# A cached-attention decode step with a gated mixer: mixer moved and cut into pieces, value products collected by four heads, repeated weight loads dropped

## The chip, the cores and the metric

The kernel runs on one core of one Trainium2 chip. The metric is the device time of one execution in microseconds (us), as a median over several runs. The span in a profile, from the first to the last instruction, is about 1.8 us shorter than that time. Not all rounds ran on the same chip.

Engines: PE is TensorE (matmuls), PEld its weight loads, DVE is VectorE, ACT is ScalarE, SP issues most loads.

## The reference, cut to what matters

One token attends to 32 heads of 16384 cached keys and values (128 wide, bf16), and a small gated mixer is added to the result:

```python
q = (x @ wq) per head                        # x: 1 x 512
scores = q . k_cache * 128 ** -0.5           # 32 heads x 16384 keys x 128
o = softmax(scores) @ v_cache                # 32 heads x 16384 values x 128
a = concat(o) @ wo
z = gelu(x @ w_in); z1, z2 = halves of z     # 512 x 1792
b = (z1 * (w_sp * layernorm(z2) + b_sp)) @ w_out
g = sigmoid(sum(x * gate_w))
return g * a + (1 - g) * b
```

Every key and value is used once: 2 x 134 MB of cache plus some 11 MB of weights are read, 279.58 MB in all.

## The kernel before

Each head has a 4 MB key tile and a 4 MB value tile, 32 KB in each of the 128 SBUF partitions. There are three key buffers and two value buffers. DVE multiplies a key tile by the query, TensorE sums the products over the head dimension with identity weights, DVE reduces what is left, ACT takes the exponential, and TensorE multiplies the values. SP issues a load as soon as its buffer is free (in the chain of before the value load at 141.92 us comes 0.02 us after the last matmul on its buffer).

```python
def load_k(h):
    t = kv.tile([P, NJ * Dh], BF16, name="k_t", tag="k", bufs=3)
    nc.sync.dma_start(out=t[:], in_=k_src[h])
...
eps_t = const.tile([P, 1], FP32, name="eps_t")       # a constant tile; it matters below
...
def scores_half(h, s):                                # two halves per head
    nc.vector.tensor_tensor(out=ks, in0=ks, in1=qh, op=ALU.mult)      # 4.4 us
    for i in range(NS):                               # 16 matmuls, all with weights ident
        nc.tensor.matmul(s_ps[:, :, :], lhsT=ident[:, :], rhs=ks[:, :, i * W:(i + 1) * W], ...)
    nc.vector.tensor_reduce(out=s_sb[...], in_=s_ps[:, :, :], axis=AX.X, op=ALU.add)
    if s == 1: nc.scalar.activation(out=p_t[:], in_=s_sb[:], func=ACT.Exp, ...)

def attend_wide(h):                                   # 32 matmuls of 4 x 512, one copy
    for g in range(NG):
        nc.tensor.matmul(d_ps[:, :], lhsT=p_sb[h][:, g * R:(g + 1) * R],
                         rhs=vtile[h][:, g * R * Dh:(g + 1) * R * Dh], ...)
    nc.scalar.copy(out=d_sb[:], in_=d_ps[:, :])
def collect(h):                                       # 4 small matmuls per head
    ...
with tc.manual_schedule(engines={PE}):                # program order on PE, DVE left to the scheduler
    for h in range(H - 1):
        ... load_k(h + AHEAD); load_v(h)
        scores_half(h + AHEAD, 0); collect(h - 1); scores_half(h + AHEAD, 1); attend_wide(h)
        if h == 1:
            gate()
            mixer()
```

The two large mixer weights (2.75 MB) are loaded right after the first value tile. The last three heads use 128 matmuls of one column each in place of `attend_wide`, and the 4 MB of output weights come last, in four pieces.

The softmax here doesn't subtract the row's maximum and nothing guards it: scores larger than these inputs give would overflow.

## Time and profile before

| | before |
|---|---|
| time, median of 5 | 662.9 us |
| span in the profile | 661.8 us |
| read from HBM | 279.58 MB, 422 GB/s over the span |
| PE, PEld, DVE, ACT busy | 80%, 35%, 50%, 6% |

The page of the kernel before: the first two lines are busy tenths of the DMA engines and GB/s in 40 equal slices, then two DMA queues (packets, MB, share of the 16 engines), then the chain that ended last by engine, then three groups (busy us, mean ns of one, idle before it and what ended the idle time).

```profile
DMA  9999999899999999999999999999999999999996
GB/s 380 440 417 444 418 441 427 360 425 440 429 426 441 426 431 434 427 434 427 432 437 426 433 434 425 436 425 438 429 430 436 429 430 435 428 433 430 431 414 250
...
q1 hardware_dynamic: 10520, 279.58, 98.5%
q8 instruction: 22, 0.36, 0.2%
...
DMA 60%; PE 30%; DVE 9%; SPq 1%; issue 0%; ACT 0%; DVEq 0%
...
L222 DVE TENSOR_TENSOR k_t<-k_t,qb 128x8192 bf16<-128x8192 bf16 x64 | 280.5, 4421 | 137.1 <-DMA k_t<-in_A_k_cache_dram 137.1
L225 PE MATMUL s_ps<-k_t,ident 128*128 128x512 bf16 x1024 | 268.6, 423 | 95.3 <-DVE k_t L222 95.3
...
L225 PEld LDWEIGHTS <-ident 128*128 128x128 bf16 x1024 | 106.4, 107 | 243.4 <-issue 148.7
```

The DMA engines are busy nearly all the time, and the compute engines wait for key tiles. The chain view shows PE for 30%, but that is not PE limiting: a load in the chain waits in the DMA queue behind earlier loads (a key tile took 36.8 us from issue to landing, and its 4 MB alone would take an estimated 9.7 us at the 431 GB/s of the windows), so the chain passes through whatever freed its buffer some 37 us earlier. The one visible dent is the slice with 360 GB/s. The windows view shows it closer; the columns are the stretch, then its length and the busy time of PE, PEld, DVE, ACT and POOL (with instruction counts), the granted clock, the DMA share and GB/s.

```profile
120.00:124.00 4.00, 4.00 (x20) 1.56 (x19) 4.00 (x2) 1.68 (x3) 0.00 (x0) 1.00 0.93 401
124.00:128.00 4.00, 4.00 (x19) 1.54 (x18) 4.00 (x2) 0.57 (x1) 0.00 (x0) 1.00 0.73 254
128.00:132.00 4.00, 4.00 (x23) 2.23 (x22) 1.89 (x2) 0.00 (x0) 0.00 (x0) 1.00 0.73 303
132.00:136.00 4.00, 4.00 (x20) 1.60 (x19) 1.07 (x2) 0.34 (x2) 0.00 (x0) 1.00 1.10 475
200.00:300.00 100.00, 83.51 (x367) 35.34 (x365) 50.63 (x20) 4.88 (x15) 0.00 (x0) 0.93 1.01 432
300.00:400.00 100.00, 83.35 (x377) 35.37 (x375) 51.23 (x21) 5.28 (x17) 0.00 (x0) 0.95 1.00 430
```

The timeline tells why (start, duration, engine, line, operation; in brackets the idle time before it). The first three lines are value loads being issued, the others the mixer.

```profile
92.07 0.33 SPq L85 DMA_DIRECT2D v_t<-in_A_v_cache_dram  x1
...
126.82 0.33 SPq L85 DMA_DIRECT2D v_t<-in_A_v_cache_dram  x1
...
141.92 0.33 SPq L85 DMA_DIRECT2D v_t<-in_A_v_cache_dram  x1
```

```profile
98.79 4.42 DVE L222 TENSOR_TENSOR k_t<-k_t,qb 128x8192 bf16<-128x8192 bf16 x1
...
103.20 4.40 DVE L222 TENSOR_TENSOR k_t<-k_t,qb 128x8192 bf16<-128x8192 bf16 x1
107.52 0.28 DVE L195 TENSOR_SCALAR z2n<-z,mv,rstd 128x7 f32<-128x7 f32 x1
...
108.65 0.89 PE L207 MATMUL a_ps<-u,w_out 128*128 128x1 bf16 x28 [10.37 <-DVE u L202]
```

The mixer's short vector chain sits behind two long key products, PE stands still for 10.4 us in front of the mixer's last matmuls, the value buffer is freed late, and two value loads are issued 34.8 us apart where about 19.4 us is the usual spacing. The DMA queue runs dry: by the packet records nothing at all moved from 127.4 to 127.8 us.

### The profile page before, as it was taken

What the parts mean: (1) busy time and instruction counts of PE and PEld (TensorE: products, weight loads), DVE (VectorE), ACT (ScalarE), POOL (GpSimd) and SP (SyncE); (2) the same over time, 40 slices, a digit from 0 to 9 for tenths busy, and PEclk for the clock granted to TensorE, in tenths of its full rate; (3) what the DMA queues carried; (4) which work ended last, traced back from release to release, by engine and by line L of the source; (5) the groups of instructions that cost most, each with busy time, mean ns of one, the idle gap of its engine ahead of it and who ended that gap; (6) DMA issues with size and microseconds to landing.
All of it is one profiled execution on the core that took longest, in us unless ns stands there. A gap on an engine that the chain in (4) does not pass through costs nothing.

```text
span 661.8 us, 6195 instructions
## 1 busy us (share of the span) xinstructions
PE 528.6 (80%) x2835; PEld 234.3 (35%) x2835; DVE 329.8 (50%) x164; ACT 39.5 (6%) x108; POOL 0.7 (0%) x6
## 2 busy tenths in 40 slices
PE   2777584999887898788799878789878879987884
PEld 1233242444332343333233333234333333333453
DVE  1592515666564445555444656444555544465600
ACT  0200020100000000000000000000000000000000
POOL 0000000000000000000000000000000000000000
PEclk9799595999899989889998988998988999897965
DMA  9999999899999999999999999999999999999996
GB/s 380 440 417 444 418 441 427 360 425 440 429 426 441 426 431 434 427 434 427 432 437 426 433 434 425 436 425 438 429 430 436 429 430 435 428 433 430 431 414 250
DMA packets 10554, 279.98 MB, mean 423 GB/s; under 512 B 1182, under 2 KB 1184, under 8 KB 1568
## 3 DMA queue, kind: packets, MB, share of 16 engines
q1 hardware_dynamic: 10520, 279.58, 98.5%
q8 instruction: 22, 0.36, 0.2%
q14 instruction: 4, 0.03, 0.0%
q10 hardware_dynamic: 8, 0.00, 0.0%
HBM read 279.58 MB, written 0.00 MB: 422 GB/s over the span
## 4 chain that ended last, share of the span: by engine, by line
DMA 60%; PE 30%; DVE 9%; SPq 1%; issue 0%; ACT 0%; DVEq 0%
DMA k_t<-in_A_k_cache_dram 52%; PE s_ps L225 15%; PE d_ps L250 12%; DVE k_t L222 8%; DMA v_t<-in_A_v_cache_dram 4%; DMA wo_t<-in_A_wo_dram 4%; PE o_ps L259 2%; SPq L85 1%; PE o_ps L239 1%; PE z_ps L167 0%; PE a_ps L317 0%; PE a_ps L207 0%; SPq L293 0%; PE tot_ps L184 0%; SPq L69 0%
## 5 line engine op out<-in xcount | busy, mean ns | idle before, releaser
L222 DVE TENSOR_TENSOR k_t<-k_t,qb 128x8192 bf16<-128x8192 bf16 x64 | 280.5, 4421 | 137.1 <-DMA k_t<-in_A_k_cache_dram 137.1
L225 PE MATMUL s_ps<-k_t,ident 128*128 128x512 bf16 x1024 | 268.6, 423 | 95.3 <-DVE k_t L222 95.3
L250 PE MATMUL d_ps<-v_t,p_t 128*4 128x512 bf16 x928 | 205.0, 379 | 0.0
L225 PEld LDWEIGHTS <-ident 128*128 128x128 bf16 x1024 | 106.4, 107 | 243.4 <-issue 148.7
L250 PEld LDWEIGHTS <-p_t 128*4 128x4 bf16 x928 | 76.4, 85 | 126.1 <-issue 12.3
L227 DVE TENSOR_REDUCE s_sb<-s_ps 128x64 f32<-128x512 f32 x64 | 44.2, 690 | 148.1 <-PE s_ps L225 148.1
L231 ACT ACTIVATE p_t<-s_sb 128x128 bf16<-128x128 f32 x32 | 9.9, 309 | 385.5 <-DVE s_sb L227 385.5
L259 PEld LDWEIGHTS o_ps<-ident_f,d_sb 4*128 4x128 f32 x232 | 27.9, 186 | 12.3 <-issue 12.3
L259 PE MATMUL o_ps<-ident_f,d_sb 4*128 4x1 f32 x232 | 30.4, 248 | 0.0
L254 ACT COPY d_sb<-d_ps 4x512 f32<-4x512 f32 x29 | 16.7, 574 | 170.7 <-PE d_ps L250 170.7
L121 PE MATMUL q_ps<-wq_t,xb 128*128 128x512 bf16 x32 | 9.7, 477 | 10.3 <-DMA wq_t<-in_A_wq_dram 10.3
L239 PE MATMUL o_ps<-p_t,v_t 128*128 128x1 bf16 x384 | 10.8, 165 | 4.1 <-DMA v_t<-in_A_v_cache_dram 4.1
L239 PEld LDWEIGHTS <-v_t 128*128 128x128 bf16 x384 | 10.5, 102 | 4.5 <-DMA v_t<-in_A_v_cache_dram 4.5
L121 PEld LDWEIGHTS <-xb 128*128 128x128 bf16 x32 | 3.7, 117 | 16.0 <-issue 12.9
L207 PE MATMUL a_ps<-u,w_out 128*128 128x1 bf16 x28 | 0.9, 165 | 10.4 <-DVE u L202 10.4
L317 PE MATMUL a_ps<-o,wo_t 128*128 128x1 bf16 x128 | 3.9, 166 | 4.4 <-DMA wo_t<-in_A_wo_dram 4.4
L124 DVE CAST qb<-q_ps 128x512 bf16<-128x512 f32 x1 | 0.7, 692 | 11.0 <-PE q_ps L121 11.0
L231 ACT ACTIVATION_READ_ACCUMULATOR p_t<-s_sb 128x1 f32 x32 | 6.0, 186 | 0.0
L317 PEld LDWEIGHTS <-wo_t 128*128 128x128 bf16 x128 | 3.6, 104 | 4.6 <-DMA wo_t<-in_A_wo_dram 4.6
L304 DVE TENSOR_TENSOR o_sb<-o_ps,rl 128x32 bf16<-128x32 f32 x1 | 0.2, 192 | 10.1 <-PE o_ps L239 10.1
L126 ACT CAST qb<-q_ps 128x512 bf16<-128x512 f32 x7 | 4.1, 585 | 15.9 <-PE q_ps L121 15.9
L207 PEld LDWEIGHTS <-w_out 128*128 128x128 bf16 x28 | 1.1, 111 | 10.4 <-issue 10.4
(65 smaller groups left out, 24.8 us busy)
## 6 DMA issues: line engine op xcount, KB each, us to landing
k_t<-in_A_k_cache_dram SPq DMA_DIRECT2D x32, 4096.0 KB, 36.8
v_t<-in_A_v_cache_dram SPq DMA_DIRECT2D x31, 4096.0 KB, 27.4
wq_t<-in_A_wq_dram SPq DMA_DIRECT2D x1, 4096.0 KB, 12.2
v_t<-in_A_v_cache_dram SPq DMA_DIRECT2D x1, 2048.0 KB, 11.1
v_t<-in_A_v_cache_dram SPq DMA_DIRECT2D x2, 1024.0 KB, 14.4
wo_t<-in_A_wo_dram SPq DMA_DIRECT2D x1, 2048.0 KB, 20.9
w_in<-in_B_w_in_dram SPq DMA_DIRECT2D x1, 1792.0 KB, 44.6
wo_t<-in_A_wo_dram SPq DMA_DIRECT2D x1, 1024.0 KB
```

The source lines that it names most:

```text
L85: nc.sync.dma_start(out=t[:, a * Dh:b * Dh], in_=v_src[h][:, a * Dh:b * Dh])
L121: nc.tensor.matmul(q_ps[:, :], lhsT=xb[:, c, :], rhs=wq[:, c, nb * QB:(nb + 1) * QB], start=(c == 0), stop=(c == DC - 1))
L126: nc.scalar.copy(out=qb[:, nb * QB:(nb + 1) * QB], in_=q_ps[:, :])
L222: nc.vector.tensor_tensor(out=ks, in0=ks, in1=qh, op=ALU.mult)
L225: nc.tensor.matmul(s_ps[:, :, :], lhsT=ident[:, :], rhs=ks[:, :, i * W:(i + 1) * W], start=(i == 0), stop=(i == NS - 1))
L227: nc.vector.tensor_reduce(out=s_sb[:, s * NH:(s + 1) * NH], in_=s_ps[:, :, :], axis=AX.X, op=ALU.add)
L231: nc.scalar.activation(out=p_t[:], in_=s_sb[:], func=ACT.Exp, scale=inv_sqrt_dh, accum_out=L_sb[:, h:h + 1])
L239: nc.tensor.matmul(o_ps[:, h:h + 1], lhsT=v3[:, j, :], rhs=p_sb[h][:, j:j + 1], start=(j == 0), stop=(j == NJ - 1))
L250: nc.tensor.matmul(d_ps[:, :], lhsT=p_sb[h][:, g * R:(g + 1) * R], rhs=vtile[h][:, g * R * Dh:(g + 1) * R * Dh], start=(g == 0), stop=(g = ...
L254: nc.scalar.copy(out=d_sb[:], in_=d_ps[:, :])
L259: nc.tensor.matmul(o_ps[:, h:h + 1], lhsT=diag[h][:, r * Dh:(r + 1) * Dh], rhs=ident_f[:, r:r + 1], start=(r == 0), stop=(r == R - 1))
L317: nc.tensor.matmul(a_ps[:, c:c + 1], lhsT=wo4[:, k, c, :], rhs=o2[:, k:k + 1], start=False, stop=(k == H - 1), skip_group_check=True)
```

## The change

Its intent is to take the mixer out of PE's way and to do less work on PE and ACT. It has five parts: (1) gate and mixer are cut into pieces, put between the vector products of heads 22 to 24, and their weights are loaded at head 19; (2) DVE too gets a fixed order, both products of a head and then both reductions; (3) four heads share one PSUM bank, 32 partitions apart, with one drain copy and one collect per four heads; (4) a pass over the finished instruction list drops weight loads that repeat the weights already loaded; (5) a constant tile grows from 1 to 121 columns although one column is used.

```diff
-    eps_t = const.tile([P, 1], FP32, name="eps_t")
-    nc.vector.memset(eps_t[:], 1e-5)
+    eps_t = const.tile([P, 121], FP32, name="eps_t")
+    nc.vector.memset(eps_t[:, 0:1], 1e-5)
 ... (mixer loads moved into load_mixer(), with four tiny loads; mixer cut into functions)
+    def scores_mult(h):
+        for ks in halves(h):
+            nc.vector.tensor_tensor(out=ks, in0=ks, in1=qh, op=ALU.mult)
 ... (scores_sum, scores_exp: the rest of scores_half)
     def attend_wide(h):
+        d_ps = d_banks[(h // G) % 2]
+            nc.tensor.matmul(d_ps[32 * g:32 * g + R, :], lhsT=p_sb[h][:, t * R:(t + 1) * R], ...)
+    def drain(h0): ...      # one copy of 128 x 512 per four heads
+    def collect(h0, n): ... # four matmuls per four heads
-    with tc.manual_schedule(engines={mybir.EngineType.PE}):
+    MIX = 22
+    dve_extra = {MIX: [gate_x], MIX + 1: [gate_out, mixer_gelu], MIX + 2: [mixer_norm]}
+    pe_extra = {MIX: [gate_ps, mixer_z], MIX + 1: [mixer_tot], MIX + 2: [mixer_out]}
+    with tc.manual_schedule(engines={mybir.EngineType.PE, mybir.EngineType.DVE}):
 ...
+def _drop_repeated_loads(nc):
+    for block in nc.m.functions[0].blocks:
+        held, keep = None, []
+        for i in block.instructions:
+            if isinstance(i, mybir.InstLdweights):
+                what = repr(i.ins[0]), i.tile_position, i.tile_size
+                ...
+                if what == held and bare:       # bare: it neither waits nor signals
+                    continue
+                held = what
 ...
```

More of the change, by code (lines that the diff above doesn't have):

```diff
@@ L60 @@
     x_row = const.tile([1, D], BF16, name="x_row")
-    gw_row = const.tile([1, D], BF16, name="gw_row")
-    wb_row = const.tile([1, 2], BF16, name="wb_row")
     nc.scalar.dma_start(out=x_row[:], in_=A_x.rearrange("b s d -> (b s) d"))
-    nc.scalar.dma_start(out=gw_row[:], in_=gate_w.rearrange("(a d) -> a d", a=1))
-    nc.scalar.dma_start(out=wb_row[:, 0:1], in_=B_w_sp)
-    nc.scalar.dma_start(out=wb_row[:, 1:2], in_=B_b_sp.rearrange("(a d) -> a d", a=1))
     wq_t = kv.tile([P, DC * HDh], BF16, name="wq_t", tag="v")
@@ L100 @@
     load_v(0)
-    w_in = const.tile([P, DC, F], BF16, name="w_in")
-    nc.sync.dma_start(out=w_in[:].rearrange("p c f -> p (c f)"),
-                      in_=B_w_in.rearrange("(p c) f -> p (c f)", c=DC))
-    w_out = const.tile([P, FhC, D], BF16, name="w_out")
-    nc.sync.dma_start(out=w_out[:].rearrange("p k n -> p (k n)"),
-                      in_=B_w_out.rearrange("(p k) n -> p (k n)", k=FhC))
     xb_ps = ps_m.tile([P, DC * P], FP32, name="xb_ps", tag="mm")
@@ L132 @@
                               in_=ident[0:H, 0:H])
-    ident_f = const.tile([4, 4], FP32, name="ident_f")
-    nc.vector.tensor_copy(out=ident_f[:], in_=ident[0:4, 0:4])
+    pick = const.tile([P, 4, 4], FP32, name="pick")
+    nc.vector.tensor_copy(out=pick[:].rearrange("p r g -> p g r"),
+                          in_=ident[:].rearrange("p (g m) -> p g m", m=32)[:, :, 0:4])
+    d_banks = [ps_1.tile([P, 512], FP32, name=f"d_ps{i}") for i in range(2)]
+    for t in d_banks:
+        nc.vector.memset(t[:, :], 0.0)
     a_ps = ps_1.tile([P, 512], FP32, name="a_ps")
@@ L141 @@
     wbf = const.tile([P, 2], FP32, name="wbf")
-    def gate():
-        gw_ps = ps_m.tile([P, DC + 2], FP32, name="gw_ps", tag="mm")
-        for c in range(DC):
-            nc.tensor.matmul(gw_ps[:, c:c + 1], lhsT=gw_row[0:1, c::DC], rhs=ones_row[0:1, 0:1],
-                             start=True, stop=True)
-        nc.tensor.matmul(gw_ps[:, DC:DC + 2], lhsT=ones_row[0:1, :], rhs=wb_row[0:1, :],
-                         start=True, stop=True)
-        gw_col = const.tile([P, DC], BF16, name="gw_col")
-        nc.vector.tensor_copy(out=gw_col[:], in_=gw_ps[:, 0:DC])
-        nc.vector.tensor_copy(out=wbf[:], in_=gw_ps[:, DC:DC + 2])
-        g_ps = ps_m.tile([P, 1], FP32, name="g_ps", tag="mm")
-        for c in range(DC):
-            nc.tensor.matmul(g_ps[:, :], lhsT=xb[:, c, :], rhs=gw_col[:, c:c + 1],
-                             start=(c == 0), stop=(c == DC - 1))
-        nc.scalar.activation(out=g_sb[:], in_=g_ps[:, :], func=ACT.Sigmoid)
-        nc.scalar.activation(out=gm_sb[:], in_=g_ps[:, :], func=ACT.Sigmoid, scale=-1.0)
@@ L162, in mixer, with load_mixer @@
-    def mixer():
+    w_in = const.tile([P, DC, F], BF16, name="w_in")
+    w_out = const.tile([P, FhC, D], BF16, name="w_out")
+    xg = const.tile([8, 2, D // 8], BF16, name="xg")
+    wb_row = const.tile([1, 2], BF16, name="wb_row")
+    def load_mixer():
+        nc.sync.dma_start(out=w_in[:].rearrange("p c f -> p (c f)"),
+                          in_=B_w_in.rearrange("(p c) f -> p (c f)", c=DC))
+        nc.sync.dma_start(out=xg[:, 0, :], in_=A_x.rearrange("b s (p d) -> (b s p) d", p=8))
+        nc.sync.dma_start(out=xg[:, 1, :], in_=gate_w.rearrange("(p d) -> p d", p=8))
+        nc.sync.dma_start(out=wb_row[:, 0:1], in_=B_w_sp)
+        nc.sync.dma_start(out=wb_row[:, 1:2], in_=B_b_sp.rearrange("(a d) -> a d", a=1))
+        nc.sync.dma_start(out=w_out[:].rearrange("p k n -> p (k n)"),
+                          in_=B_w_out.rearrange("(p k) n -> p (k n)", k=FhC))
@@ new lines, with gate_x, gate_ps @@
+    branch = {}
+    def gate_x():
+        xgp = const.tile([8, D // 8], BF16, name="xgp")
+        nc.vector.tensor_mul(out=xgp[:], in0=xg[:, 0, :], in1=xg[:, 1, :])
+        xgs = const.tile([8, 1], FP32, name="xgs")
+        nc.vector.reduce_sum(out=xgs[:], in_=xgp[:], axis=AX.X)
+        branch["xgs"] = xgs
+    def gate_ps():
+        xgs = branch["xgs"]
+        g_ps = ps_m.tile([P, 3], FP32, name="g_ps", tag="mm")
+        nc.tensor.matmul(g_ps[:, 0:1], lhsT=ones_f[0:8, :], rhs=xgs[:, :], start=True, stop=True)
+        nc.tensor.matmul(g_ps[:, 1:3], lhsT=ones_row[0:1, :], rhs=wb_row[0:1, :],
+                         start=True, stop=True)
+        branch["g_ps"] = g_ps
@@ L163, in mixer, with gate_out, mixer_z @@
+    def gate_out():
+        g_ps = branch["g_ps"]
+        nc.vector.tensor_copy(out=wbf[:], in_=g_ps[:, 1:3])
+        nc.scalar.activation(out=g_sb[:], in_=g_ps[:, 0:1], func=ACT.Sigmoid)
+        nc.scalar.activation(out=gm_sb[:], in_=g_ps[:, 0:1], func=ACT.Sigmoid, scale=-1.0)
+    z = const.tile([P, FC], FP32, name="z")
+    stats = const.tile([P, 2], FP32, name="stats")
+    u = const.tile([P, FhC], BF16, name="u")
+    def mixer_z():
         z_ps = ps_m.tile([P, FC], FP32, name="z_ps", tag="mm")
@@ L168, in mixer, with mixer_gelu @@
                                  rhs=xb[:, c, 0:1], start=(c == 0), stop=(c == DC - 1))
-        z = const.tile([P, FC], FP32, name="z")
-        nc.vector.tensor_copy(out=z[:], in_=z_ps[:])
+        branch["z_ps"] = z_ps
+    def mixer_gelu():
+        nc.vector.tensor_copy(out=z[:], in_=branch["z_ps"][:])
         t = const.tile([P, FC], FP32, name="t")
@@ L177, in mixer @@
         nc.vector.tensor_mul(out=z[:], in0=z[:], in1=t[:])
-        stats = const.tile([P, 2], FP32, name="stats")
         nc.vector.reduce_sum(out=stats[:, 0:1], in_=z[:, FhC:FC], axis=AX.X)
@@ L182, in mixer, with mixer_tot, mixer_norm @@
         nc.vector.reduce_sum(out=stats[:, 1:2], in_=sq[:], axis=AX.X)
+    def mixer_tot():
         tot_ps = ps_m.tile([P, 2], FP32, name="tot_ps", tag="mm")
         nc.tensor.matmul(tot_ps[:, :], lhsT=ones_f[:, :], rhs=stats[:, :], start=True, stop=True)
+        branch["tot"] = tot_ps
+    def mixer_norm():
+        tot_ps = branch["tot"]
         mv = const.tile([P, 2], FP32, name="mv")
@@ L200, in mixer, with mixer_out @@
         nc.vector.tensor_mul(out=uf[:], in0=z[:, 0:FhC], in1=z2n[:])
-        u = const.tile([P, FhC], BF16, name="u")
         nc.vector.tensor_scalar(out=u[:], in0=uf[:], scalar1=gm_sb[:, 0:1], scalar2=0.0,
                                 op0=ALU.mult, op1=ALU.add)
+    def mixer_out():
         w_out4 = w_out[:].rearrange("p k (c m) -> p k c m", c=DC)
@@ L211, with halves, scores_sum @@
     p_sb = {}
-    s_tile = {}
-    def scores_half(h, s):
+    s_part = {}
+    def halves(h):
         k3 = ktile[h][:].rearrange("p (j d) -> p j d", d=Dh)
+        return [k3[:, s * NH:(s + 1) * NH, :] for s in range(2)]
+    def scores_mult(h):
         qh = qb[:, h * Dh:(h + 1) * Dh].unsqueeze(1).broadcast_to([P, NH, Dh])
-        if s == 0:
-            s_tile[h] = sp.tile([P, NJ], FP32, name="s_sb")
-        s_sb = s_tile[h]
-        ks = k3[:, s * NH:(s + 1) * NH, :]
-        nc.vector.tensor_tensor(out=ks, in0=ks, in1=qh, op=ALU.mult)
+        for ks in halves(h):
+            nc.vector.tensor_tensor(out=ks, in0=ks, in1=qh, op=ALU.mult)
+    def scores_sum(h, s):
+        ks = halves(h)[s]
         s_ps = ps_s.tile([P, NH, W], FP32, name="s_ps")
@@ L226, in scores_half, with scores_exp @@
                              start=(i == 0), stop=(i == NS - 1))
-        nc.vector.tensor_reduce(out=s_sb[:, s * NH:(s + 1) * NH], in_=s_ps[:, :, :],
-                                axis=AX.X, op=ALU.add)
-        if s == 1:
-            p_t = sp.tile([P, NJ], BF16, name="p_t", bufs=4)
-            nc.scalar.activation(out=p_t[:], in_=s_sb[:], func=ACT.Exp, scale=inv_sqrt_dh,
-                                 accum_out=L_sb[:, h:h + 1])
-            p_sb[h] = p_t
+        s_part[h, s] = s_ps
+    def scores_exp(h):
+        s_sb = sp.tile([P, NJ], FP32, name="s_sb")
+        for s in range(2):
+            nc.vector.tensor_reduce(out=s_sb[:, s * NH:(s + 1) * NH], in_=s_part[h, s][:, :, :],
+                                    axis=AX.X, op=ALU.add)
+        p_t = sp.tile([P, NJ], BF16, name="p_t", bufs=4)
+        nc.scalar.activation(out=p_t[:], in_=s_sb[:], func=ACT.Exp, scale=inv_sqrt_dh,
+                             accum_out=L_sb[:, h:h + 1])
+        p_sb[h] = p_t
     def attend(h):
@@ L243 @@
     R = 512 // Dh
+    G = 4
     diag = {}
     def attend_wide(h):
-        d_ps = ps_s.tile([R, R * Dh], FP32, name="d_ps")
+        g = h % G
+        d_ps = d_banks[(h // G) % 2]
         NG = NJ // R
-        for g in range(NG):
-            nc.tensor.matmul(d_ps[:, :], lhsT=p_sb[h][:, g * R:(g + 1) * R],
-                             rhs=vtile[h][:, g * R * Dh:(g + 1) * R * Dh],
-                             start=(g == 0), stop=(g == NG - 1))
-        d_sb = sp.tile([R, R * Dh], FP32, name="d_sb")
@@ L254, in attend_wide, with drain @@
-        nc.scalar.copy(out=d_sb[:], in_=d_ps[:, :])
-        diag[h] = d_sb
-    def collect(h):
+        for t in range(NG):
+            nc.tensor.matmul(d_ps[32 * g:32 * g + R, :], lhsT=p_sb[h][:, t * R:(t + 1) * R],
+                             rhs=vtile[h][:, t * R * Dh:(t + 1) * R * Dh],
+                             start=(t == 0), stop=(t == NG - 1))
+    def drain(h0):
+        d_sb = sp.tile([P, R * Dh], FP32, name="d_sb", bufs=1)
+        nc.scalar.copy(out=d_sb[:], in_=d_banks[(h0 // G) % 2][:, :])
+        diag[h0] = d_sb
@@ L258, in collect @@
+    def collect(h0, n):
         for r in range(R):
-            nc.tensor.matmul(o_ps[:, h:h + 1], lhsT=diag[h][:, r * Dh:(r + 1) * Dh],
-                             rhs=ident_f[:, r:r + 1], start=(r == 0), stop=(r == R - 1))
+            nc.tensor.matmul(o_ps[:, h0:h0 + n], lhsT=diag[h0][:, r * Dh:(r + 1) * Dh],
+                             rhs=pick[:, r, 0:n], start=(r == 0), stop=(r == R - 1))
     AHEAD = 2
     WIDE = H - 3
-    with tc.manual_schedule(engines={mybir.EngineType.PE}):
+    MIX = 22
@@ L265 @@
+    dve_extra = {MIX: [gate_x], MIX + 1: [gate_out, mixer_gelu], MIX + 2: [mixer_norm]}
+    pe_extra = {MIX: [gate_ps, mixer_z], MIX + 1: [mixer_tot], MIX + 2: [mixer_out]}
+    due = None
+    with tc.manual_schedule(engines={mybir.EngineType.PE, mybir.EngineType.DVE}):
         for h in range(AHEAD):
-            scores_half(h, 0)
-            scores_half(h, 1)
+            scores_mult(h)
+            scores_sum(h, 0)
+            scores_sum(h, 1)
+            scores_exp(h)
         for h in range(H - 1):
+            ahead = h + AHEAD if h + AHEAD < H else None
@@ L269 @@
             if h > 0:
-                if h + AHEAD < H:
-                    load_k(h + AHEAD)
+                if ahead is not None:
+                    load_k(ahead)
                 load_v(h)
-            if h + AHEAD < H:
-                scores_half(h + AHEAD, 0)
-            if 0 < h <= WIDE:
-                collect(h - 1)
+            if h == MIX - 3:
+                load_mixer()
+            if ahead is not None:
+                scores_mult(ahead)
+            for f in dve_extra.get(h, ()):
+                f()
@@ L277 @@
+            if ahead is not None:
+                scores_sum(ahead, 0)
+            if due is not None:
+                collect(*due)
+                due = None
             if h < WIDE:
-                scores_half(h + AHEAD, 1)
+                scores_sum(ahead, 1)
                 attend_wide(h)
+                if h % G == G - 1 or h == WIDE - 1:
+                    drain(h - h % G)
+                    due = (h - h % G, h % G + 1)
             else:
                 attend(h)
-                if h + AHEAD < H:
-                    scores_half(h + AHEAD, 1)
@@ L284 @@
-            if h == 1:
-                gate()
-                mixer()
+                if ahead is not None:
+                    scores_sum(ahead, 1)
+            if ahead is not None:
+                scores_exp(ahead)
+            for f in pe_extra.get(h, ()):
+                f()
         load_v(H - 1, cuts=(64, 96))
@@ L325 @@
     nc.sync.dma_start(out=out.rearrange("a b (c m) -> (a b c) m", c=DC), in_=resT[:])
+def _drop_repeated_loads(nc):
[4 more added lines that the diff above has]
+                what = repr(i.ins[0]), i.tile_position, i.tile_size
+                s = i.sync_info
+                bare = s is None or not (list(s.on_wait) or list(s.on_update))
+                if what == held and bare:
+                    continue
+                held = what
+            elif isinstance(i, mybir.InstMatmult) and i.ldweights is not False:
+                held = None
+            keep.append(i)
+        block.instructions[:] = keep
 _INS = ['A_x', 'A_k_cache', 'A_v_cache', 'A_wq', 'A_wo', 'B_x', 'B_w_in', 'B_w_sp', 'B_b_sp', 'B_w_out', 'gate_w']
@@ L352 @@
         kernel(tc, *args)
+    _drop_repeated_loads(nc)
     r = _run(nc, [arrays], core_ids=[0])
```

## The prediction

> **What bounds the kernel now.** The loads. In the windows view every stretch from 140 to 600 us has a DMA share of 1.00 and 430 to 432 GB/s, while PE is busy about 83% and DVE about 51%.[...] At 431 GB/s the 279.58 MB read take 648.7 us. The span is 661.8, so 13 us are lost in all. By the windows view:
> - start, 0 to 6 us (197, 295, 295 GB/s): 2.3 us;
> - 124 to 132 us (254 and 303 GB/s): 2.8 us;
> - the last small output-weight pieces, 652 to 658 us (356, 216, 80 GB/s): 3.0 us;
> - after the last load (landed about 657.8): 4.0 us of final matmuls, copies and the store.
>
> **The hole at 124 to 132 us** comes from the gate and mixer after head 1. In the timeline the mixer starts at 92, its vector chain is caught behind two 4.4 us key products (98.8 to 107.6), and PE waits 10.4 us for u. The next value load is issued at 126.8, 34.8 us after the one before, where the steady spacing is 19.4: the queue has run dry.
>
> **What the change does.**
> - Gate and mixer move to heads 22 to 24, in pieces between the vector products, with their 2.75 MB loaded at head 19. In steady state values take 27.4 us from issue to landing (DMA issues), against 9.7 us of transfer: some 18 us of queued work hide the pieces (estimated from the timeline: 4 us on PE, 5 on DVE). The hole vanishes, no new one opens: 2.8 us gained.
> - Those 2.75 MB no longer fill the queue at the start (6.4 us). From the first heads' durations I estimate the third value load to be issued at about 70 us, with the queue full until about 82. The vector order (both products, then both reductions) costs a few us inside that margin. 0 us.
> - Repeated identity loads dropped (106 us of weight-load time, nearly all overlapped), collects once per four heads (30.4 us of PE to an estimated 4 to 8), drains once per four heads (16.7 us of ACT to about 4.6): PE then only waits longer for loads. 0 us.
> - Four tiny loads join the main queue: at most a few tenths lost.
> - Start and tail are unchanged.
>
> Elsewhere the critical path is the loads: the removed work is off it.
>
> **Prediction:** 660.1 us, 658.6 to 661.8 in 8 of 10 cases; faster by over 2%: 0.02, within 2%: 0.97, slower: 0.01.
>
> **What would show it.** Windows at 120 to 140 us at about 430 GB/s and no hole at heads 22 to 24 (about 450 to 530 us); steady windows still 430 to 432; weight-load busy time from 234 to roughly 110 us, PE down by about 25, ACT by about 12. The last load lands 2.8 us earlier; the 4.0 us after it stay.
>
> **What would make it wrong.** The queue runs dry at the start, because the filler is gone and the vector order delays the first releases (a hole near 75 to 95 us); DVE's strict order makes it wait for PE at heads 22 to 24; the DMA rate depends on what the engines do in SBUF (the steady rate would move); the tiny loads hold up one DMA engine; or PE at half clock stretches the tail.

662.9 us less 2.8 us for the hole is 660.1 us; the other terms were put at 0 (the tiny loads at a few tenths at most, not in the sum). The "half clock" of its last paragraph is in the windows of before: the granted clock was 0.50 from 100 to 112 us and from 652 us to the end.

## The result

| | before | after |
|---|---|---|
| time, median | 663.32 us (13 runs) | 656.85 us (7 runs, 656.67 to 657.10) |
| span | 661.8 us | 655.0 us |
| PE, PEld, DVE, ACT busy | 528.6, 234.3, 329.8, 39.5 us | 514.7, 110.5, 331.6, 28.2 us |

The ratio is 0.9906, with a 95% interval of 0.9896 to 0.9916. (A ratio is the mean time of one kernel's runs over that of the other's in the same rounds, so it is not quite the ratio of the medians.) The prediction was 660.1 us, 658.6 to 661.8: right in sign and in the 2% class, but the gain is 6.5 us where about 2.8 was forecast, and the time lies outside the range.

The same lines of the page of the kernel after:

```profile
DMA  9999999999999999999999999999999999999996
GB/s 384 428 436 429 434 432 431 438 426 439 424 439 425 438 426 437 432 440 427 436 427 437 430 437 427 425 438 441 422 442 423 438 431 438 425 438 428 435 417 286
...
q1 hardware_dynamic: 10556, 279.58, 99.1%
q8 instruction: 17, 0.28, 0.2%
...
DMA 61%; PE 28%; DVE 9%; SPq 1%; issue 0%; DVEq 0%
...
L253 PE MATMUL s_ps<-k_t,ident 128*128 128x512 bf16 x1024 | 277.4, 436 | 116.6 <-DVE k_t L247 116.6
L247 DVE TENSOR_TENSOR k_t<-k_t,qb 128x8192 bf16<-128x8192 bf16 x64 | 280.3, 4421 | 158.8 <-DMA k_t<-in_A_k_cache_dram 158.8
...
L253 PEld LDWEIGHTS <-ident 128*128 128x128 bf16 x38 | 4.3, 114 | 19.1 <-issue 10.5
```

The windows of the kernel after:

```profile
124.00:128.00 4.00, 2.62 (x7) 0.00 (x0) 4.00 (x2) 0.00 (x0) 0.00 (x0) 0.65 0.97 418
128.00:132.00 4.00, 4.00 (x23) 1.07 (x9) 2.35 (x2) 0.00 (x0) 0.00 (x0) 0.93 1.04 451
132.00:136.00 4.00, 4.00 (x20) 0.51 (x7) 0.69 (x1) 0.36 (x2) 0.00 (x0) 1.00 1.02 442
200.00:300.00 100.00, 80.12 (x339) 15.79 (x183) 53.87 (x22) 2.52 (x12) 0.00 (x0) 0.91 1.00 432
300.00:400.00 100.00, 81.92 (x336) 14.72 (x174) 53.78 (x21) 2.49 (x11) 0.00 (x0) 0.89 1.01 434
```

The hole is gone. The chain is as before: loads 61%. Identity weight loads fell from 1024 to 38 and PE waits some 20 us longer for products. The long windows are 0 to 4 GB/s faster, which is hardly visible there, and the instruction queue q8 has 17 packets where it had 22.

A better way to see where time was gained is to ask each trace when the same number of bytes had landed. The following is worked out from the packet records of the two traces (load queue only; us from the span's start):

```
MB landed     before     after    gained so far
    50        119.31    118.78      0.53
    60        145.50    141.83      3.67
   200        470.32    465.72      4.60
   270        632.97    627.81      5.16
   279        654.23    648.63      5.60
   end        658.02    651.34      6.68
```

The step between 50 and 60 MB is the hole, about 3.1 us. A slow drift runs through the whole kernel: from 60 to 270 MB the rate is 430.8 GB/s before and 432.1 after, 1.5 us. And another 1.5 us comes in the last 10 MB. The prediction had only the first of these three.

The packet records also show what the drift is. Each key or value tile is moved in 128 packets of 32 KB, one per partition; shared evenly, that is eight for each of the 16 DMA engines. Durations of these packets between 150 and 600 us:

```
            1213 ns   others             mean
before        25%     up to 1765 ns      1217.9 ns
after        99.6%    up to 1764 ns      1214.1 ns
```

Of the packets of before 73% took 1214 to 1222 ns.

### The profile page after: what moved, and what is told of

Same layout as the page of the kernel before. It is cut to its first block, busy times and chain, and to the rows that moved or that the text cites. A ratio compares the mean times of both kernels' runs of the same rounds, so it can differ in the third digit from the quotient of the medians.

```text
span 655.0 us, 4851 instructions
## 1 busy us (share of the span) xinstructions
PE 514.7 (79%) x2661; PEld 110.5 (17%) x1675; DVE 331.6 (51%) x167; ACT 28.2 (4%) x88; POOL 0.7 (0%) x6
## 2 busy tenths in 40 slices
DMA packets 10579, 279.90 MB, mean 427 GB/s; under 512 B 1213, under 2 KB 1214, under 8 KB 1598
## 4 chain that ended last, share of the span: by engine, by line
DMA 61%; PE 28%; DVE 9%; SPq 1%; issue 0%; DVEq 0%
DMA k_t<-in_A_k_cache_dram 58%; PE s_ps L253 16%; PE d_ps L285 11%; DVE k_t L247 9%; DMA wo_t<-in_A_wo_dram 3%; SPq L80 1%; PE o_ps L271 0%; PE o_ps L296 0%; DVE s_sb L260 0%; PE a_ps L372 0%; SPq L348 0%; SPq L64 0%; PE tot_ps L204 0%; PE rT_ps L377 0%; DVE resT L379 0%
## 5 line engine op out<-in xcount | busy, mean ns | idle before, releaser
L253 PE MATMUL s_ps<-k_t,ident 128*128 128x512 bf16 x1024 | 277.4, 436 | 116.6 <-DVE k_t L247 116.6
L296 PEld LDWEIGHTS o_ps<-pick,d_sb 128*128 128x128 f32 x64 | 8.4, 192 | 67.3 <-issue 67.1
L291 ACT COPY d_sb<-d_ps 128x512 f32<-128x512 f32 x8 | 4.7, 585 | 168.2 <-PE d_ps L285 168.2
L296 PE MATMUL o_ps<-pick,d_sb 128*128 128x4 f32 (+1 forms) x64 | 7.6, 242 | 0.0
L253 PEld LDWEIGHTS <-ident 128*128 128x128 bf16 x38 | 4.3, 114 | 19.1 <-issue 10.5
L184 PE MATMUL z_ps<-xb,w_in 128*128 128x1 bf16 x56 | 3.1, 192 | 0.0
```

The lines of the kernel that those rows point to most:

```text
L291: nc.scalar.copy(out=d_sb[:], in_=d_banks[(h0 // G) % 2][:, :])
L296: nc.tensor.matmul(o_ps[:, h0:h0 + n], lhsT=diag[h0][:, r * Dh:(r + 1) * Dh], rhs=pick[:, r, 0:n], start=(r == 0), stop=(r == R - 1))
```

## The experiments

Theory. The gain has three parts: (A) no hole, about 2 to 3 us; (B) the tile of part 5 is a pad. It moves every key and value buffer (the query and output weights use them too; the mixer weights do not) from 128 bytes past a multiple of 512 bytes in each SBUF row (the first value buffer lay at 52864 = 103 x 512 + 128) onto one (52736 = 103 x 512; these are the SBUF addresses of the built programs), and packets to a better aligned place are shorter, 2 to 2.5 us; (C) fewer instructions mean fewer instruction fetches (17 packets of q8 where there were 22), which use the same DMA engines, about 1.3 us at the end.

Rivals. The rate rose because TensorE reads fewer weights from SBUF; weight loads cost nothing at all; the late place of the mixer, not its cutting, removed the hole.

Twelve kernels were run (four to six timed runs each); all gave correct results. Where an edit is to "before" or "after", nothing else differs.

### The place of the buffers

**Kernel before, padded (e1).**

```diff
-    eps_t = const.tile([P, 1], FP32, name="eps_t")
+    eps_t = const.tile([P, 97], FP32, name="eps_t")     # only column 0 is set and used
```

> The kernel before, with one constant tile padded so that every key, value and weight buffer starts 384 bytes higher in each SBUF row: on a multiple of 512 bytes, as in the kernel after, where before it was 128 bytes past one. Nothing else differs. Alignment theory: the 32 KB load packets take 1213 ns nearly all, as after (mean 1214), not 1213 to 1222 (mean 1218), the rate from 60 to 270 MB goes from 430.8 to about 432.1 GB/s, and the time falls by 2 to 2.5 us to about 661. Rival (the rate rose because TensorE reads fewer weights, or fewer instructions are fetched by DMA): packets stay at a mean of 1218 ns and the time stays within 0.5 us of before. The hole at 124 to 132 us stays in both.

Measured: 660.8 us (659.24 to 661.42), ratio to before 0.9972 (0.9957 to 0.9986). Of the packets 99% take 1213 ns, mean 1214.2; the rate from 60 to 270 MB is 432.1 GB/s; 22 fetches, as before. By the medians that is 1.4 us below the before of its rounds, by the ratio 1.9 us: the packets did what was expected, the time a little less than the 2 to 2.5 us. (e2, whose runs scatter less, measures the size better.) The hole is still there:

```profile
124.00:128.00 4.00, 4.00 (x20) 1.64 (x19) 3.60 (x1) 0.58 (x1) 0.00 (x0) 1.00 0.76 262
128.00:132.00 4.00, 4.00 (x23) 2.21 (x22) 0.69 (x1) 0.00 (x0) 0.00 (x0) 1.00 1.08 459
```

**Kernel after, moved to the old place (e2).**

```diff
-    eps_t = const.tile([P, 121], FP32, name="eps_t")
+    eps_t = const.tile([P, 153], FP32, name="eps_t")    # buffers 128 bytes past a multiple of 512
```

> The kernel after, with the same pad grown by 128 bytes, so that the buffers lie where they lay before, 128 bytes past a multiple of 512. Alignment theory: packets back to a mean of about 1218 ns, time up by 2 to 2.5 us to about 659. Rival (fewer weight loads, fewer instruction fetches): 656.9 us and a mean of 1214 ns as after.

Measured: 659.23 us (659.07 to 659.49), 2.38 us above after; packets 1213 to 1222 ns, mean 1218.0; 430.5 GB/s; 17 fetches. With all of after's savings of work kept, the packets are those of before. So the place of the buffers, and not the work on the engines, made the packet time here: a mean of 1218 ns at 128 bytes past a multiple of 512 in both kernels, 1214 ns at a multiple. The rival that the rate depends on weight reads falls with these two runs, and with e4 below.

**How much alignment is needed (e8, e11).** Two more places for the kernel after.

```diff
+    eps_t = const.tile([P, 185], FP32, name="eps_t")    # 256 bytes past a multiple of 512
```

> The kernel after with the buffers 256 bytes past a multiple of 512. If the packets need buffers on a multiple of 256 bytes, they stay at 1213 ns and the time at 656.9; if it must be 512, they go to 1213 to 1222 ns and the time to about 659.2, as at 128 bytes.

Measured: 656.9 us, mean packet 1214.0 ns: as after (656.85 us, 1214.1 ns). So 256 bytes past a multiple of 512 costs nothing that shows.

```diff
+    eps_t = const.tile([P, 1], FP32, name="eps_t")      # the change without its pad: 32 bytes past
```

> The kernel after with the pad taken out of its constant tile, so that the buffers lie 32 bytes past a multiple of 512. If a place off a 256-byte multiple costs the same everywhere: 659.2 us, packets at a mean of 1218 ns. If it costs more off a 64-byte multiple, packets are longer than 1222 ns and the time is over 660.

Measured: 659.87 us (659.84 to 659.97), 3.0 us above after. Most packets take 1216 ns, 22% take 1224, mean 1219.0. The guess of one equal cost was a little low. Of the other guess, the longer packets came, but only for some, and the time "over 660" was not reached. The change without its pad would have lost about half of its gain.

So the place is shown to be the cause of the longer packets: at 0 and 256 bytes past a multiple of 512 they take a mean of 1214.1 and 1214.0 ns, at 128 and 32 bytes past it 1218.0 and 1219.0 ns. How it lengthens them was not shown.

### The instruction fetches

**Kernel after with the repeated weight loads back (e4).**

```diff
-    _drop_repeated_loads(nc)
```

> The kernel after without the pass that drops repeated weight loads, so some 960 weight loads come back. Theory that they are off the critical path but their instructions are fetched by the same DMA engines: weight-load busy time back up by about 100 us, fetches of 16 KB from 17 to about 21, time up by 0.3 to 1.2 us to 657.2 to 658.1. Rival (weight loads cost nothing at all): 656.9. Rival (they set the load rate by reading SBUF): up by 2 us or more with packets at 1218 ns.

Measured: 658.1 us (657.99 to 658.27), 1.25 us above after, with packets still at 1213 ns (mean 1214.2) and 21 fetches. The page has both:

```profile
q8 instruction: 21, 0.34, 0.2%
...
L253 PEld LDWEIGHTS <-ident 128*128 128x128 bf16 x1024 | 110.8, 109 | 280.1 <-issue 182.3
```

So 106 us less of busy time on the weight loader is worth 1.25 us. Is it the loads themselves or the fetching of their instructions? The next run tells a slope from a staircase.

**Kernel after with every second repeated load kept (e5).**

```diff
                 if what == held and bare:
-                    continue
+                    seen += 1
+                    if seen % 2:
+                        continue
```

> The kernel after with every second of the repeated weight loads kept (493 more TensorE instructions[...] than after, half as many as in the run that kept all). Fetch theory: 16 KB instruction fetches fall in turn on 8 of the 16 DMA engines and delay each by about 1.4 us; the slowest engine ends the kernel. After has 16 fetches before its last load lands (2 on each of the 8), keeping all 20 (3 on four of them). Half should have 18 (3 on two of them): the same slowest engine as with all, so a step: about 658.1 us, with two engines landing last. Rival (each weight load costs a little, in proportion): 657.5 us. Rival (loads are free, the last run's difference was chance): 656.9.

Measured: 658.28 us (658.07 to 658.40). Half of the loads cost as much as all of them: a step. The packet records show the step directly. For each DMA engine, this is the time at which its last packet of the last piece of output weights landed (us from the span's start, sorted). The trace names no engine; packets are put down to one when each starts where another ends:

```
after          648.0 648.2 648.3 648.4 648.6 648.7 648.7 649.8 | 650.7 650.8 650.9 651.0 651.1 651.1 651.3 651.3
  (16 fetches before the end)                                     8 engines
half kept      648.1 648.4 648.4 648.4 648.5 648.7 648.8 650.1 | 650.9 651.0 651.1 651.2 651.2 651.2 | 652.5 652.6
  (18 fetches)                                                    6 engines                            2 engines
all kept       648.0 648.1 648.1 648.2 648.2 648.7 648.8 650.0 | 650.9 651.0 651.0 651.1 | 652.4 652.6 652.6 652.7
  (20 fetches)                                                    4 engines                4 engines
```

Put down in this way, each of the 16 engines of the kernel after carries 512 packets of 32 KB, give or take two: the same bytes of cache, as near as this method tells. Eight of them end about 2.7 us late with 16 fetches, and each two further fetches move two engines back by another 1.4 us. The reading of these times: each fetch of 16 KB delays one engine by about 1.4 us and they go round eight engines in turn: 16 = 8 x 2, 18 = 8 x 2 + 2, 20 = 8 x 2 + 4. The last landing then moves by a step when some engine gets its third fetch: 651.3 us with 16 fetches, 652.6 with 18, 652.7 with 20. (The one engine near 650 us is unexplained.) In single packets: a fetch itself took 0.88 to 0.99 us in the kernel after, and one 32 KB packet right after it took 1.68 to 1.76 us where its neighbours took 1.213; fetch and excess together are the 1.4 us. That the fetches go round eight engines is inferred, from these end times and from one thing more: the durations of the packets right after the first eight fetches, 1681, 1681, 1693, 1762, 1764, 1707, 1711 and 1719 ns, come again in nearly the same order after the next six (1681, 1681, 1694, 1764, 1762, 1707).

By the counts of the two profiles 986 more instructions (2661 weight loads against 1675) went with four more fetches of 16 KB (21 against 17), an estimate of about 250 instructions for each fetch. Their cost is not hidden in this kernel, which is bound by loads: it is the 1.25 us of e4.

**Kernel before with the dropping pass alone (e6).**

```diff
+    _drop_repeated_loads(nc)
```

> The kernel before with only the pass that drops repeated weight loads added. Fetch theory: fetches from 22 to about 18, at most 2 instead of 3 on one DMA engine after the hole at 124 to 132 us, where all engines wait and the differences between them vanish: about 1.2 us less than before, near 661.3; packets stay at 1218 ns and the hole stays. Theory that weight loads cost nothing: as before, 662.5. Theory that they set the load rate: packets at 1214 ns and 2 us or more gained.

Measured: 660.9 us (660.64 to 661.44), ratio 0.9977 (0.9962 to 0.9991), 1.4 us below before by the medians; 18 fetches, mean packet 1217.7 ns, and the hole is there (279 GB/s in the window 124 to 128 us). As the fetch theory expected (about 1.2 us): the time falls, the packets and the hole stay.

### The hole

**Kernel before, mixer late but in one piece (e3).**

```diff
-            if h == 1:
+            if h == 22:
                 gate()
                 mixer()
     # and the loads of w_in and w_out moved from after load_v(0) to after load_v(19)
```

> The kernel before with gate and mixer in one piece as they were, but after head 22 instead of head 1, and their two large loads after the value load of head 19. Hole theory: the queue is deep there, the hole at 124 to 132 us vanishes and the time falls by 2.5 to 3 us to about 660.4; packets stay at 1218 ns. If a new hole opens near 480 us, cutting the mixer into pieces was needed too and the gain is smaller.

Measured: 660.99 us, ratio 0.9978 (0.9966 to 0.9990), 1.2 us below the before of its rounds. In the profile the hole near 128 us is gone (442 and 401 GB/s) and 3.2 us were gained by 60 MB, but 0.8 us of it were lost again between 220 and 240 MB: two value loads, at 498.8 and 533.0, are again 34 us apart. The gain is under half of the 2.5 to 3 us expected. This was ambiguous; the run with three small edits (e12) settles it.

**Kernel after, mixer early but in pieces (e7).**

```diff
-    MIX = 22
+    MIX = 1
-            if h == MIX - 3:
-                load_mixer()
+    load_mixer()                       # right after the first value load
```

> The kernel after with gate and mixer still in pieces, but at heads 1 to 3 and with their loads right after the first value load, as before. If cutting them into pieces between the vector products was enough, no hole opens between 100 and 140 us and the time stays within 0.5 us of after, 656.9. If the late place was needed, a hole of 2 to 3 us comes back and the time is about 659.5.

Measured: 656.94 us (656.82 to 656.99), as after. No hole:

```profile
100.00:120.00 20.00, 16.33 (x69) 2.95 (x35) 11.57 (x12) 3.26 (x5) 0.00 (x0) 0.91 1.00 431
120.00:140.00 20.00, 17.21 (x96) 4.50 (x70) 10.15 (x4) 2.27 (x4) 0.00 (x0) 0.83 1.00 432
```

Given the new order, the late place is worth nothing.

**Three small edits on before (e12):** padded as in the first run, mixer late in one piece, repeated loads dropped (the three diffs above together).

> The kernel before with three small edits only: buffers on a multiple of 512 bytes, gate and mixer in one piece but after head 22, repeated weight loads dropped; no pieces, no vector order, collects and drains per head as before. From the single edits (1.9, 1.3 to 1.5 and 1.4 us) it should take about 657.6 us, within 1 us of after: then the rest of the change (pieces, vector order, collects and drains by four) is worth at most 1 us. If it stays above 658.5, the rest matters more.

Measured: 659.76 us (658.19 to 660.23), not 657.6. The single gains did not add up. The windows of this kernel show why:

```profile
526.00:530.00 4.00, 4.00 (x20) 0.85 (x11) 2.01 (x2) 0.40 (x2) 0.00 (x0) 1.00 1.06 455
530.00:534.00 4.00, 4.00 (x20) 1.60 (x19) 4.00 (x2) 0.00 (x0) 0.00 (x0) 1.00 0.55 238
534.00:538.00 4.00, 4.00 (x20) 0.28 (x4) 3.35 (x1) 0.57 (x1) 0.00 (x0) 1.00 0.56 172
538.00:542.00 4.00, 4.00 (x23) 1.06 (x9) 0.69 (x1) 0.00 (x0) 0.00 (x0) 1.00 1.14 492
```

The mixer in one piece opens the same hole at head 22, now at 530 to 538 us; between 220 and 240 MB landed it falls 3.3 us behind after. (In e3 a gap of 34 us between value loads cost only 0.8 us; why was not studied.) The wait of PE that starts it is the same as in before. These lines are of e12:

```profile
506.89 4.42 DVE L224 TENSOR_TENSOR k_t<-k_t,qb 128x8192 bf16<-128x8192 bf16 x1
...
511.30 4.41 DVE L224 TENSOR_TENSOR k_t<-k_t,qb 128x8192 bf16<-128x8192 bf16 x1
...
516.75 0.89 PE L209 MATMUL a_ps<-u,w_out 128*128 128x1 bf16 x28 [10.36 <-DVE u L204]
```

PE waits 10.4 us for `u`, the end of the mixer's vector chain, in before, e3 and e12. In after, e7 and e10 it does not wait for it: `u` is written at 526.6 us and first used at 536.9 in after, at 118.8 and 128.3 in e7. So what closed the hole is the new order, wherever the mixer stands. By these waits it is the cutting into pieces with a fixed vector order; which of the two matters more was not separated, and no run took the rest of the restructuring (the gate computed on DVE, collects and copies for four heads at once) away from them.

### Does the sum close?

**Kernel after, unchanged, in the last rounds (e9).**

> The kernel after, unchanged, as the yardstick of these rounds: 656.9 us.

Measured: 656.82 us.

**Kernel after without its pad's effect and with all weight loads (e10).**

```diff
+    eps_t = const.tile([P, 153], FP32, name="eps_t")
-    _drop_repeated_loads(nc)
```

> The kernel after without its two side effects: buffers back at 128 bytes past a multiple of 512, repeated weight loads kept. What is left is the restructuring (gate and mixer late and in pieces, vector order, one collect per four heads). If the three terms add up (2.4 us for the place of the buffers, 1.25 us for the instruction fetches), it takes about 660.5 us, which is what the prediction on record gave for the whole change: packets at 1218 ns, 20 fetches before the last load, no hole. If the terms overlap, it lies below 660.

Measured: 660.72 us (660.58 to 660.77), ratio 0.9966 (0.9952 to 0.9979); mean packet 1218.2 ns, 20 fetches before the end. The restructuring alone gives 662.77 - 660.72 = 2.05 us by the medians of its rounds (by the ratio about 2.3, with an interval of 1.4 to 3.2).

In the profiled spans it is 2.8 us (661.8 to 659.0), but the profiled execution of before (663.59 us) was one of its slowest. It took 26.2 us between 50 and 60 MB; e1 and e6, which have the hole too, took 24.8 and 24.6, and after 23.1. So the hole cost 3.1 us in that execution and about half of it in the two others. Only the kernels with a hole of more than 1 us (before, e1, e6, e12) scatter by more than 0.4 us; a hole that varies would explain it, which was not tested.

Then the place of the buffers (2.38 us, from e2) and the fetches (1.25 us, from e4) add 3.63 us, and the measured step from this kernel to after is 660.72 - 656.82 = 3.90 us. Nearly all of the gain in these rounds, 662.77 - 656.82 = 5.95 us, is accounted for. (The 6.5 us of the first rounds are against a median of before that was 0.55 us higher.)

No run beat after: e7, e8 and e9 lie between 656.82 and 656.94 us. The eight DMA engines that end 2.7 us early are room that no kernel here uses; whether they can be given more of the load was not tried.

## Why the prediction was wrong

- *"The hole vanishes, no new one opens: 2.8 us gained."* Right that it vanishes and that none opens. The size was read from one slow execution: the restructuring alone gave 2.05 us by medians, and 2.8 us only against that execution. The reason named more than was needed. The prediction counted on the 18 us of queued work at heads 19 to 24 to hide the pieces. Run e12 shows that this depth does not cover a mixer in one piece, and e7 that the pieces need no late place.
- *"steady windows still 430 to 432"* failed. This was the silent term of the sum: the load rate was taken as fixed at 431 GB/s, and all other work as off the critical path. Part 5 of the change, a tile grown to 121 columns for no visible use, was in the diff and was passed over. It shortens the packets from a mean of 1218 to 1214 ns, which is worth 2.4 us. A list of what could go wrong had "the DMA rate depends on what the engines do in SBUF"; the rate did move, but for another reason. Read in stretches of 100 us the windows (432 and 434 after, 432 and 430 before) hardly show it; the durations of single packets do.
- *"Repeated identity loads dropped ... 0 us"* failed by 1.25 us. It is true that the loads are overlapped: PEld fell from 234 to 110.5 us, as forecast. What was missed is that instructions too are loaded by the very engines that bound the kernel, in blocks of 16 KB (21 against 17 for 986 instructions more), and that the engine that ends last counts (652.7 us against 651.3).
- *The start.* The third value load was estimated at about 70 us and was issued at 72.4; no hole opened at 75 to 95 us. Right.
- *PE down by about 25 us, ACT by about 12.* ACT fell by 11.3. PE fell only by 13.9: the collects fell from 30.4 to 7.6 us as forecast, but the score matmuls grew from 423 to 436 ns on average. The mean granted clock went from 0.906 to 0.893 at the same time; whether that is the reason was not tested.
- *"The last load lands 2.8 us earlier; the 4.0 us after it stay."* It landed 6.7 us earlier; what comes after it hardly changed (3.8 us before, 3.7 after).

With the two missed terms left out of the kernel (e10), the time was 660.72 us, inside the range and 0.6 us from its centre.

## What to carry to other kernels

When a kernel is bound by loads, price everything in DMA time: where the buffers start (here a mean of 1214 ns a packet at 0 or 256 bytes past a multiple of 512, 1218 and 1219 ns at 128 and 32 bytes past it) and how many instructions are fetched (here 1.25 us for four more fetches), not only the bytes of the tensors. Look at single packet durations and at when each DMA engine ends, since an average rate hides both. An odd line in a diff, such as a tile larger than its use, is a reason to ask what it moves. And a short chain of dependent small operations can be caught between long ones: here the new order with the chain in pieces removed the wait, while moving the chain as a whole moved the hole with it.
